# Top-32 attention with a highway layer: the 32nd value joins the common maximum, and GpSimd's part of a step is ordered anew

## The chip, the cores and the metric

The kernel runs on one core of a Trainium2 chip. The metric is the device time of one execution in microseconds (us), of the slowest core, which is here the only one. Five engines work side by side, each in the order of its own queue: TensorE (PE in the profile, its weight loads PEld), VectorE (DVE), ScalarE (ACT), GpSimd (POOL) and SyncE (SP), which here issues DMAs. They wait for each other by semaphores.

## The reference

Attention over 8 batches and 8 heads of 576 queries and keys (64 numbers each), in which only the 32 largest scores of a row count, followed by a highway layer over 4608 tokens of 512 numbers:

```python
scores = scale * np.matmul(q, k.transpose(0, 1, 3, 2))
kth = np.partition(scores, -32, axis=-1)[..., -32:-32 + 1]
scores = np.where(scores >= kth, scores, -1000000000.0)
attn = np.exp(scores - np.max(scores, axis=-1, keepdims=True))
x = np.matmul(attn / (np.sum(attn, axis=-1, keepdims=True) + 1e-09), v)   # then tokens x 512
H = np.maximum(x @ w_h, 0.0)
T = 1.0 / (1.0 + np.exp(-(x @ w_t + b_t)))
out = T * H + (1.0 - T) * x
```

Only the 32nd largest score of each row and its largest are needed, not the sorted list.

## The kernel before

**Units and steps.** A unit is 128 rows of scores: one head and one of four full blocks of 128 queries, or two heads and the remaining 64 queries. There are 288 units in 144 pairs, 18 pairs to a batch. The main loop calls `step(i)` for i = 0 to 142, and `finish` handles the last pair. Every engine's instructions run in the order in which the program writes them; there is no planner, so a line moved in `step` is moved in the queue of its engine.

**The 32nd largest value.** For each unit VectorE takes the eight largest of each of six segments of 96 scores (L353, `cand`, twelve instructions a pair). `refine` (L366 to L382) makes from them a threshold that is at or below the 24th largest value and near it: a maximum and a minimum of neighbouring segments (`high` L366, `low` L368), the negated `high` (`neg` L370), the eight largest of `low` and of `neg` for each unit (L373, L376, `en`), and their combination into a column of `cand` (L378). L382 is a maximum over `cand` in two groups: it writes the largest score (TOP) and the threshold (THR) of both units into `wall`. ScalarE then compares all scores with the threshold (L397, `masks_of`), which gives a mask and a count of the row (`csum`). PE adds the mask onto the scores in PSUM, so that all scores above the threshold sink (L410), and VectorE takes the eight largest of what remains (L420, `below`). With the count it is known which of the nine values, threshold and eight followers, is the 32nd: L426 compares nine constants with the count (`hits`: one 1 and eight 0), GpSimd multiplies these with the nine values (L436, `pick_a`), and VectorE sums the nine products (L439, `pick_b`) into the column KTH of `wall`.

**The use of it.** GpSimd's L391 (`biases`) multiplies TOP and KTH with factors for ScalarE's functions; the program makes it wait for VectorE's last keeping instruction of the step. For the first unit of a pair ScalarE makes the exponentials (L416) and a large value for every score above the 32nd (L443, `above`), and VectorE takes their minimum (L450). For the second GpSimd compares the scores with the 32nd (L454, `above_one`, `ro`), and VectorE multiplies (L460). When five or more passes of the layer wait for GpSimd, L454 is left out and VectorE does both at once (L465). SyncE's DMAs transpose the result, and PE multiplies it with v.

**Stages side by side.** Step i holds, of pair i+1, the segments (L353) and `refine`; of pair i, L420, L416, L426, L436 and L439; of pair i-1, L443, L454, L450 and L460; of pair i-3, the product with v; and PE starts the scores of pair i+2 (L309 and L318; L326 and L335 for the remaining 64 queries) in the buffer that pair i leaves.

**The layer.** When a block of queries is complete, `norm` takes it over: VectorE adds a constant to the sums (L557) and takes reciprocals (L559), and GpSimd scales (L564). GpSimd casts it by a DMA (L582), SyncE transposes it by another (L587), PE multiplies with the weights, and ScalarE evacuates the products (L609, L633). GpSimd makes three more passes over 128x512 or 128x256 numbers (L610, L611, L624), and a DMA of its own queue adds the results (L694, `do_add`). Other DMAs of that queue load v and the weights (L176, L182, L187, L213). The passes stand in a list, `pool_work`; `do_work` takes from its front what fits in the width that it is given. In `step`, the order on GpSimd is L391 of the step before, L454, the passes, L436, then DMAs, then L391. The evacuation of the layer's product stands ahead of `do_work` and appends the passes that it allows.

**Flags.** At the end `finish` checks on the chip that each 32nd value is positive, that each largest value is in a safe range and that the threshold lay where it should; otherwise a slower path computes everything again.

Of the kernel before, what the change touches and what calls it, by code (L numbers as in the profile page):

```python
# [10 lines left out]
ALU = mybir.AluOpType  # L11
# [15 lines left out]
def kernel(  # L27
# [68 lines left out]
    for jj in range(NPK):  # L96
        nc.vector.memset(pidx[:, jj : jj + 1], S - 2.0 * (TOP_K - jj))

    TOP, THR, KTH = 0, 1, NPK + 1
    wall = consts.tile([P, NU + 2, NPK + 2], FP32)  # L100
    fac = consts.tile([P, 2, 2], FP32)
    nc.vector.memset(fac[:, :, 0], -scale)
# [6 lines left out]
        nc.vector.memset(en[:, 0, :, 0:1], 3.0e38)  # L109
        ends.append(en)  # L110
    csum = consts.tile([P, NU], FP32)
    nc.vector.memset(wall[:, 0:2, KTH : KTH + 1], 0.0)

    def kth(u):
        return wall[:, u + 2, KTH : KTH + 1]
# [6 lines left out]

    cands = []
    for i in range(4):
        cand = consts.tile([P, 2, 8, 8], FP32, name=f"cand{i}")
        nc.vector.memset(cand[:, :, NSEG:, 0:1], -3.0e38)
        cands.append(cand)
    NM = 4
    masks = []
# [228 lines left out]
    def refine(g, cand):  # L358
        u0, u1 = pairs[g][0], pairs[g][1] + 1
        en = ends[g % NE]  # L360
        one = cand[:, :, 0:NSEG:2, :]
        two = cand[:, :, 1:NSEG:2, ::-1]
        high = cpool.tile([P, 2 * HALF], FP32, name="high")
        low = cpool.tile([P, 2 * HALF], FP32, name="low")
        neg = cpool.tile([P, 2 * HALF], FP32, name="neg")
        nc.vector.tensor_tensor(high[:].rearrange("p (s k r) -> p s k r", s=2, r=8), one, two, ALU.max)  # L366
        yield
        nc.vector.tensor_tensor(low[:].rearrange("p (s k r) -> p s k r", s=2, r=8), one, two, ALU.min)  # L368
        yield
        nc.vector.tensor_scalar(neg[:], high[:], -1.0, None, ALU.mult)  # L370
        yield
        for s in range(2):
            nc.vector.max(en[:, 0, s, 1:9], low[:, s * HALF : (s + 1) * HALF])  # L373
            yield
        for s in range(2):
            nc.vector.max(en[:, 1, s, 0:8], neg[:, s * HALF : (s + 1) * HALF])  # L376
            yield
        nc.vector.scalar_tensor_tensor(  # L378
            out=cand[:, :, :, 1], in0=en[:, 1, :, 0:8], scalar=-1.0, in1=en[:, 0, :, 0:8], op0=ALU.mult, op1=ALU.min
        )  # L380
        yield
        nc.vector.tensor_reduce(  # L382
            wall[:, u0:u1, TOP : THR + 1],
            cand[:, :, :, 0:2].rearrange("p s r k -> p s k r"),
            mybir.AxisListType.X,
            ALU.max,
        )
        yield

    def biases(g):  # L390
        return nc.gpsimd.tensor_tensor(be[:, g], wall[:, 2 * g : 2 * g + 2, TOP : KTH + 1 : KTH - TOP], fac[:], ALU.mult)  # L391

# [22 lines left out]
        return e  # L417

    def below(u, ps):
        nc.vector.max(wall[:, u, THR + 1 : KTH], ps)  # L420


    def hits(pair):
# [7 lines left out]
        )  # L431
        return hit

    def pick_a(pair, hit):
        u0, u1 = pair[0], pair[1] + 1
        nc.gpsimd.tensor_tensor(hit[:], hit[:], wall[:, u0:u1, THR:KTH], ALU.mult)  # L436

    def pick_b(pair, hit):
        nc.vector.tensor_reduce(wall[:, pair[0] + 2 : pair[0] + 4, KTH], hit[:], mybir.AxisListType.X, ALU.add)  # L439
# [12 lines left out]
    def above_one(u, sc):  # L452
        r = epool.tile([P, S], BF16, name="ro")
        nc.gpsimd.tensor_scalar(r[:], sc, kth(u), None, ALU.is_ge)  # L454
        return r
# [93 lines left out]
    def ffn_pieces(b, qt, xs):  # L549
        nh, ng, w = shape_of(qt)  # L550
        st = dict(b=b, qt=qt, xs=xs)
        blocks.append(st)

        def norm():
            xs3 = xs[:, 0 : nh * DE].rearrange("p (h e) -> p h e", e=DE)
            rinv = cpool.tile([P, H], FP32, name="rinv")
            nc.vector.tensor_scalar(rinv[:, 0:nh], xs3[:, :, D], 1e-9, 2.0, ALU.add, ALU.mult)  # L557
            yield
            nc.vector.reciprocal(rinv[:, 0:nh], rinv[:, 0:nh])  # L559
            x = xpool.tile([P, dm], FP32, name="x")  # L560
            st["x"] = x

            def scaled(e):
                e.tensor_tensor(  # L564
                    x[:, 0:w].rearrange("p (h d) -> p h d", h=nh),
                    xs3[:, :, 0:D],
                    rinv[:, 0:nh].unsqueeze(2).to_broadcast([P, nh, D]),
                    ALU.mult,
                )
                if by_dma:  # L570
                    casts.append(cast)
                else:
                    ready.extend([xt, hh, tt])

            pool_work.append((scaled, w))
            yield

        by_dma = isinstance(b, int) and units[-1][0:2] > (b, qt + 2)

        def cast():  # L580
            xb = xpool.tile([P, dm], BF16, name="xb")
            nc.gpsimd.dma_start(xb[:, 0:w], st["x"][:, 0:w])  # L582
            return partial(turn, xb)

        def turn(xb):
            st["xT"] = fpool.tile([P, n_g, P], BF16, name="xT")
            nc.sync.dma_start_transpose(st["xT"][:, 0:ng, :], xb[:, 0:w])  # L587
            flying.append(b)
            ready.extend([hh, tt])

        def xt():
            ps = fps.tile([P, 512], FP32, tag="fp", name="fp")
            for g in range(ng):
                nc.tensor.transpose(ps[:, g * P : (g + 1) * P], st["x"][:, g * P : (g + 1) * P], ident_f[:])
            xT = fpool.tile([P, n_g, P], BF16, name="xT")
            st["xT"] = xT
            psv = ps[:].rearrange("p (g j) -> p g j", j=P)
            return lambda: nc.scalar.copy(xT[:, 0:ng, :], psv[:, 0:ng, :])

        def hh():  # L600
            ps = fps.tile([P, 512], FP32, tag="fp", name="fp")
            project(ps, qt, st["xT"], wh, False)
            h2 = hpool.tile([P, dm], FP32, name="h2")
            s1 = xpool.tile([P, dm], FP32, name="s1")
            st["h2"], st["s1"] = h2, s1
            x = st["x"]

            def evac():
                nc.scalar.activation(h2[:, 0:w], ps[:, 0:w], AF.Relu)  # L609
                pool_work.append((lambda e: e.tensor_add(s1[:, 0:w], h2[:, 0:w], x[:, 0:w]), w))  # L610
                pool_work.append((lambda e: e.tensor_sub(h2[:, 0:w], h2[:, 0:w], x[:, 0:w]), w))  # L611

            return evac

        def tt():
            ps = fps.tile([P, 512], FP32, tag="fp", name="fp")
            project(ps, qt, st["xT"], wt, True)
            if by_dma:
                flying.pop()
            t = fpool.tile([P, dm], FP32, name="tt")  # L620
            h2, s1 = st["h2"], st["s1"]

            def gated(e):
                ins = e.tensor_mul(h2[:, 0:w], h2[:, 0:w], t[:, 0:w])  # L624
                if e is nc.gpsimd:
                    adds.append((s1[:, 0:w], h2[:, 0:w], partial(store, b, qt, s1)))
                else:
                    e.tensor_add(s1[:, 0:w], s1[:, 0:w], h2[:, 0:w])
                    store(b, qt, s1)
                return ins  # L630

            def evac():
                nc.scalar.activation(t[:, 0:w], ps[:, 0:w], AF.Tanh)  # L633
                pool_work.append((gated, w))

            return evac

        return norm
# [136 lines left out]
    def step(i):  # L775
# [25 lines left out]
        if prev:  # L801
            pu, ps_ = pairs[i - 1], st[i - 1]
            ps_["r"] = [above(pu[0], ps_["sc"][0])]
            ps_["r"].append(above_one(pu[1], ps_["sc"][1]) if len(pool_work) < (3 if last_steps else 5) else None)
        if late:
            late.pop(0)()
        if back:
# [2 lines left out]
            st.pop(j)  # L810
        spare(8 if i + 2 >= NG or units[pairs[i + 2][0]][1] < nfull or po["n"] else 3)
        ev = prep_filler() if to_prep and (i <= SPB or (len(to_prep) > 15 - k_in or len(layers) > 2) and i % 2) else None
        do_work(nc.gpsimd, 2 * dm if prev and ps_["r"][1] is None else dm)
        segs(i + 1, 2 * NSEG)
        if live:
            below(pr[0], st[i]["ps"][0])
# [31 lines left out]
            ps_["et"][s] = transposes(ep)  # L848
            return ins

        for _ in range(2):
            next(ra, None)
        if live:
            hit = hits(pr)
            pick_a(pr, hit)
        added = bool(adds or casts)
        if adds:
            do_add(i)
# [3 lines left out]
            todo_v.pop(0)()  # L862
        if todo_v and (i < 5 or added and i <= SPB):
            todo_v.pop(0)()
        for _ in range(5):
            next(ra, None)
        if live:
            pick_b(pr, hit)
        next(ra, None)
        masked(0)  # L870
        for _ in ra:
            pass
        scaling = norms.pop(0)() if norms else iter(())
        next(scaling, None)
        last = masked(1)
        if live:
            after(biases(i + 1), last)
# [65 lines left out]
    def finish():  # L943
# [49 lines left out]
        hit = hits(pr)  # L993
        ep, _ = keep_min(pu[0], old["e"][0], relu)
        old["et"][0] = transposes(ep)
        nc.vector.tensor_tensor(hit[:], hit[:], wall[:, pr[0] : pr[1] + 1, THR:KTH], ALU.mult)
        pick_b(pr, hit)
        x2 = xps.tile([P, 3 * BANK], FP32, tag="x", name="xs")
        cur["et"] = [etpool.tile([P, nck, P], BF16, name="et") for s in range(2)]
# [13 lines left out]
        yb = xs_of(nfull, 0, n)  # L1013
        project(bank(x1, 0), ya["qt"], ya["xT"], wh, False)
        do_work(nc.vector, NG * dm)
        nc.vector.scalar_tensor_tensor(cond[:], wall[:, 0:NU, THR + 1], ABOVE, wall[:, 0:NU, THR], ALU.mult, ALU.add)
        while stores:
            stores.pop(0)[1]()
        sure(2, cond[:], 1.0)
# [119 lines left out]
```

## Time and profile before

| what | value |
|---|---|
| three runs | 806.29, 806.73, 807.61 us; median 806.73 |
| profiled execution | 806.17 us |
| span of its instructions | 804.5 us |
| busy: PE, DVE, ACT, POOL | 686.7, 772.8, 757.2, 559.9 us |
| DVE instructions | 4020 |
| POOL instructions | 712 |
| mean granted clock of PE | 0.996 |

The profile is one execution, recorded by the hardware. A page sums it up; further views list groups of instructions of one line (busy time, mean length of one in ns, idle time of the engine before them and what ended it), who waited for whom (total, times, longest), the chain of waits that ended last, and the timeline: start, length, engine, line, operation, what is written and read, how often, and in brackets the idle time before it. A time without a unit is in us. An instruction's line in kernel.py is written L382; `cand<-xs` means that `cand` is written and `xs` read.

### The profile page before, as it was taken

What the parts mean: (1) busy time and instruction counts of PE and PEld (TensorE: products, weight loads), DVE (VectorE), ACT (ScalarE), POOL (GpSimd) and SP (SyncE); (2) the same over time, 40 slices, a digit from 0 to 9 for tenths busy, and PEclk for the clock granted to TensorE, in tenths of its full rate; (3) what the DMA queues carried; (4) which work ended last, traced back from release to release, by engine and by line L of the source; (5) the groups of instructions that cost most, each with busy time, mean ns of one, the idle gap of its engine ahead of it and who ended that gap; (6) DMA issues with size and microseconds to landing.
All of it is one profiled execution on the core that took longest, in us unless ns stands there. A gap on an engine that the chain in (4) does not pass through costs nothing.

```text
span 804.5 us, 20583 instructions
## 1 busy us (share of the span) xinstructions
PE 686.7 (85%) x6369; PEld 494.7 (61%) x6459; DVE 772.8 (96%) x4020; ACT 757.2 (94%) x1401; POOL 559.9 (70%) x712
## 2 busy tenths in 40 slices
PE   7889998888888888888987889888888888988884
PEld 5666766566666666566665666666666566665662
DVE  5999999999999999999999999999999999999996
ACT  5999999999999999999999999999999999999984
POOL 2666867777777767777767776777776777766750
PEclk9999999999999999999999999999999999999998
DMA  6789968996799667998669766898767996555653
GB/s 121 87 137 159 134 116 140 141 143 93 140 152 148 108 96 137 154 131 125 102 135 159 125 113 107 150 156 126 112 121 136 160 124 109 90 106 110 108 90 88
DMA packets 346359, 100.37 MB, mean 125 GB/s; under 512 B 330624, under 2 KB 338432, under 8 KB 346240
## 3 DMA queue, kind: packets, MB, share of 16 engines
q1 hardware_dynamic: 291024, 79.16, 54.1%
q0 software_dynamic: 53536, 19.34, 22.6%
q8 instruction: 53, 0.87, 0.4%
q10 hardware_dynamic: 1680, 0.46, 0.3%
q14 instruction: 66, 0.54, 0.2%
HBM read 31.72 MB, written 9.44 MB: 51 GB/s over the span
## 4 chain that ended last, share of the span: by engine, by line
ACT 37%; DVE 32%; PE 23%; DMA 4%; issue 3%; SPq 1%; another core or an unknown queue 0%; DVEq 0%; ACTq 0%
ACT m L397 15%; DVE wall L420 12%; DVE cand L353 9%; ACT e L416 7%; ACT sc L348 6%; PE pso L278 5%; ACT r L443 4%; PE xs L309 4%; PE xs L326 3%; DVE ep L450 3%; DMA xT<-xb 3%; PE fp L522 3%; PE xs L410 3%; PE pso L494 2%; ACT xs L508 2%
## 5 line engine op out<-in xcount | busy, mean ns | idle before, releaser
L353 DVE MAX8 cand<-xs 128x8 f32<-128x96 f32 x1728 | 297.5, 248 | 11.4 <-PE xs L335 6.2
L278 PE MATMUL pso<-cst,ident_b 128*128 128x252 bf16 x1841 | 246.8, 272 | 42.8 <-ACT xs L508 40.4
L454 POOL TENSOR_SCALAR ro<-sc,wall 128x576 bf16<-128x576 f32 x135 | 232.8, 1724 | 0.0
L416 ACT ACTIVATE e<-sc,be 128x576 bf16<-128x576 f32 x288 | 226.5, 787 | 0.1
L278 PEld LDWEIGHTS <-ident_b 128*128 128x128 bf16 x1841 | 173.4, 98 | 81.4 <-issue 49.5
L420 DVE MAX8 wall<-xs 128x8 f32<-128x576 f32 x288 | 204.3, 751 | 5.6 <-PE xs L410 3.5
L309 PE MATMUL xs<-kT,qT 64*128 64x256 f32 x1024 | 145.3, 400 | 30.6 <-DVE high L366 26.2
L348 ACT COPY sc<-xs 128x1152 f32<-128x1152 f32 x144 | 161.0, 1118 | 0.7 <-DVE cand L353 0.6
L309 PEld LDWEIGHTS xs<-kT,qT 64*128 64x128 f32 x1024 | 93.0, 186 | 61.3 <-issue 37.6
L397 ACT ACTIVATE m<-xs,wall 128x576 int8<-128x576 f32 x144 | 107.4, 746 | 18.2 <-DVE wall L382 17.1
L436 POOL TENSOR_TENSOR hit<-hit,wall 128x18 f32<-128x18 f32 x143 | 32.4, 227 | 121.2 <-DVE hit L426 114.0
L397 ACT ACTIVATE m<-sc,wall 128x576 int8<-128x576 f32 x144 | 111.4, 773 | 0.0
L443 ACT ACTIVATE r<-sc,be 128x576 bf16<-128x576 f32 x143 | 109.9, 769 | 0.0
L410 PE MATMUL xs<-m,ident_b 128*128 128x512 bf16 (+1 forms) x512 | 92.7, 274 | 17.3 <-ACT m L397 15.2
L494 PEld LDWEIGHTS <-et 128*128 128x128 bf16 (+1 forms) x1600 | 68.6, 100 | 19.2 <-issue 3.5
L391 POOL TENSOR_TENSOR be<-wall,fac 128x4 f32<-128x4 f32 x144 | 29.2, 203 | 72.5 <-DVE ep L460 53.7
L410 PEld LDWEIGHTS <-ident_b 128*128 128x128 bf16 x576 | 51.7, 97 | 44.8 <-issue 24.1
L494 PE MATMUL pso<-vb,et 128*128 128x65 bf16 (+1 forms) x1600 | 74.4, 194 | 4.2 <-DMA et<-ep 0.3
L450 DVE TENSOR_TENSOR ep<-e,r 128x576 bf16<-128x576 bf16 x143 | 64.6, 452 | 0.2 <-ACT r L443 0.2
L318 PEld LDWEIGHTS xs<-kd,qT 128*128 128x128 f32 x256 | 38.1, 188 | 42.5 <-issue 42.1
L318 PE MATMUL xs<-kd,qT 128*128 128x128 f32 x256 | 62.5, 326 | 0.0
L460 DVE TENSOR_TENSOR ep<-e,ro 128x576 bf16<-128x576 bf16 x135 | 60.7, 449 | 0.0
(127 smaller groups left out, 1028.9 us busy)
## 6 DMA issues: line engine op xcount, KB each, us to landing
kin<-in_k_dram SPq DMA_DIRECT2D x64, 128.0 KB, 2.9
qin<-in_q_dram SPq DMA_DIRECT2D x62, 128.0 KB, 3.1
out_dram<-s SPq DMA_DIRECT2D x30, 256.0 KB, 2.8
s<-h POOLq DMA_DIRECT2D x29, 256.0 KB, 4.0
et<-ep SPq DMA_TRANSPOSE x286, 3.3
xb<-x POOLq DMA_DIRECT2D x30, 128.0 KB, 3.0
vb<-in_v_dram POOLq DMA_DIRECT2D x28, 128.0 KB, 4.8
vb<-in_v_dram POOLq DMA_DIRECT2D x24, 64.0 KB, 3.1
```

The lines of the kernel that those rows point to most:

```text
L278: nc.tensor.matmul(po["t"][:, 4 * DE : BANK], ident_b[:], cst[:, 0 : BANK - 4 * DE], start=True, stop=True, skip_group_check=True,)
L309: nc.tensor.matmul(ps[:, mo + n0 : mo + n0 + 256], qT[r : r + D, hp, qs : qs + P], kT[r : r + D, hp, n0 : n0 + 256], start=(n0 == 0), stop ...
L318: nc.tensor.matmul(ends, qT[:, hp, qs : qs + P], kd[:, hp, :], start=True, stop=True)
L348: nc.scalar.copy(sc[:], both)
L353: nc.vector.max(cand[:, s, :], sc[:, s * SEG : (s + 1) * SEG])
L397: nc.scalar.activation(m1[:].bitcast(I8)[:, 1 : 2 * S : 2], ps, AF.Sign, bias=wall[:, u, THR : THR + 1], scale=ABOVE, accum_out=csum[:, u ...
L410: nc.tensor.matmul(ps[:, s0:s1], ident_b[:], m1[:, s0:s1], start=False, stop=True, skip_group_check=True)
L416: nc.scalar.activation(e[:], sc, AF.Exp, bias=tb(u), scale=scale)
L420: nc.vector.max(wall[:, u, THR + 1 : KTH], ps)
L443: nc.scalar.activation(r[:], sc, AF.Relu, bias=eb(u), scale=BIGK)
L454: nc.gpsimd.tensor_scalar(r[:], sc, kth(u), None, ALU.is_ge)
L494: nc.tensor.matmul(pso[r0 : r0 + ql, col : col + DE], ets[s][:, c, gi * P2 : gi * P2 + ql], vb[:, h, vc, :], start=(c == 0), stop=(c == nc ...
```

## The change

Four edits, in the lines of the kernel before:

- `wall` gets the columns TOP, KTH, THR, LOW (the eight followers). `cand` gets a ninth row. L382's maximum runs over nine rows and three columns, TOP, KTH and THR, instead of eight and two: 54 numbers into 6, where it was 32 into 4.
- L439, the sum, goes. GpSimd's product (now `pick`) is written into the KTH column of the next pair's `cand`, and L382's maximum over nine rows takes the one that isn't zero. L426 moves behind the two L376, and the product with it. On GpSimd the product therefore stands behind the step's DMAs, which were behind it. On VectorE the order after L376 is L426, L378, L450, L382 (which now waits for GpSimd), L460.
- The constant of `norm` (L557) is added by GpSimd, right behind the product; the reciprocal (L559), behind L460, waits for it.
- `do_work` is called in `step` only if `pool_work` had something before the step's evacuation (always in the last eight steps); two passes in one step need more than one such.

```diff
-    TOP, THR, KTH = 0, 1, NPK + 1
+    TOP, KTH, THR, LOW = 0, 1, 2, 3
...
-    nc.vector.memset(wall[:, 0:2, KTH : KTH + 1], 0.0)
...
-        cand = consts.tile([P, 2, 8, 8], FP32, name=f"cand{i}")
-        nc.vector.memset(cand[:, :, NSEG:, 0:1], -3.0e38)
+        cand = consts.tile([P, 2, NPK, 8], FP32, name=f"cand{i}")
+        nc.vector.memset(cand[:, :, NSEG:, :], -3.0e38)
...
-            out=cand[:, :, :, 1], in0=en[:, 1, :, 0:8], scalar=-1.0, in1=en[:, 0, :, 0:8], op0=ALU.mult, op1=ALU.min
+            out=cand[:, :, 0:8, THR], in0=en[:, 1, :, 0:8], scalar=-1.0, in1=en[:, 0, :, 0:8], op0=ALU.mult, op1=ALU.min
...
-            wall[:, u0:u1, TOP : THR + 1],
-            cand[:, :, :, 0:2].rearrange("p s r k -> p s k r"),
+            wall[:, u0:u1, TOP:LOW],
+            cand[:, :, :, TOP:LOW].rearrange("p s r k -> p s k r"),
...
-    def pick_a(pair, hit):
-        u0, u1 = pair[0], pair[1] + 1
-        nc.gpsimd.tensor_tensor(hit[:], hit[:], wall[:, u0:u1, THR:KTH], ALU.mult)
+    def pick(pair, pen, cand):
+        nc.gpsimd.tensor_tensor(cand[:, :, :, KTH], pen[:], wall[:, pair[0] : pair[1] + 1, THR:], ALU.mult)
...
-            nc.vector.tensor_scalar(rinv[:, 0:nh], xs3[:, :, D], 1e-9, 2.0, ALU.add, ALU.mult)
+            nc.gpsimd.tensor_scalar(rinv[:, 0:nh], xs3[:, :, D], 1e-9, 2.0, ALU.add, ALU.mult)
...
+        old = len(pool_work)
         if late:
             late.pop(0)()
...
-        do_work(nc.gpsimd, 2 * dm if prev and ps_["r"][1] is None else dm)
+        if old or last_steps:
+            do_work(nc.gpsimd, 2 * dm if prev and ps_["r"][1] is None and old > 1 else dm)
...
-        for _ in range(2):
-            next(ra, None)
-        if live:
-            hit = hits(pr)
-            pick_a(pr, hit)
         added = bool(adds or casts)
...
-        for _ in range(5):
+        for _ in range(7):
             next(ra, None)
         if live:
-            pick_b(pr, hit)
+            pick(pr, hits(pr), st[i + 1]["cand"])
+        scaling = norms.pop(0)() if norms else iter(())
+        next(scaling, None)
         next(ra, None)
         masked(0)
         for _ in ra:
             pass
-        scaling = norms.pop(0)() if norms else iter(())
-        next(scaling, None)
         last = masked(1)
```

`finish` keeps the sum (L439) for the last pair. The generator `ra` is `refine`: seven calls of `next` reach the second L376, the eighth L378, the rest L382.

More of the change, by code (lines that the diff above doesn't have):

```diff
@@ L390, in biases @@
     def biases(g):
-        return nc.gpsimd.tensor_tensor(be[:, g], wall[:, 2 * g : 2 * g + 2, TOP : KTH + 1 : KTH - TOP], fac[:], ALU.mult)
+        return nc.gpsimd.tensor_tensor(be[:, g], wall[:, 2 * g : 2 * g + 2, TOP:THR], fac[:], ALU.mult)
     def mask_count(u, ps):
@@ L419, in below @@
     def below(u, ps):
-        nc.vector.max(wall[:, u, THR + 1 : KTH], ps)
+        nc.vector.max(wall[:, u, LOW:], ps)
     def hits(pair):
@@ L995, in finish @@
         old["et"][0] = transposes(ep)
-        nc.vector.tensor_tensor(hit[:], hit[:], wall[:, pr[0] : pr[1] + 1, THR:KTH], ALU.mult)
+        nc.vector.tensor_tensor(hit[:], hit[:], wall[:, pr[0] : pr[1] + 1, THR:], ALU.mult)
         pick_b(pr, hit)
@@ L1015, in finish @@
         do_work(nc.vector, NG * dm)
-        nc.vector.scalar_tensor_tensor(cond[:], wall[:, 0:NU, THR + 1], ABOVE, wall[:, 0:NU, THR], ALU.mult, ALU.add)
+        nc.vector.scalar_tensor_tensor(cond[:], wall[:, 0:NU, LOW], ABOVE, wall[:, 0:NU, THR], ALU.mult, ALU.add)
         while stores:
```

## The prediction

> **What bounds the kernel now.** I read the page first: its busy shares, then the chain that ended last.
>
> ```profile
> span 804.5 us, 20583 instructions
> PE 686.7 (85%) x6369; PEld 494.7 (61%) x6459; DVE 772.8 (96%) x4020; ACT 757.2 (94%) x1401; POOL 559.9 (70%) x712
> ACT 37%; DVE 32%; PE 23%; DMA 4%; issue 3%; SPq 1%; another core or an unknown queue 0%; DVEq 0%; ACTq 0%
> ```
>
> DVE and ACT are both nearly full, and the chain changes between ACT, DVE and PE. So a nanosecond taken from DVE counts only in steps where DVE ends last. The next view is therefore DVE's timeline through one ordinary step (start, length, instruction):
>
> ```profile
> 341.29 2.07 DVE L353 MAX8 cand<-xs 128x8 f32<-128x96 f32 x12 [0.23 <-PE xs L318]
> 343.28 1.41 DVE L420 MAX8 wall<-xs 128x8 f32<-128x576 f32 x2
> ...
> 344.72 0.20 DVE L368 TENSOR_TENSOR low<-cand 128x48 f32<-128x48 f32 x1
> 344.83 0.17 DVE L426 TENSOR_TENSOR hit<-pidx,csum 128x18 f32<-128x18 f32 x1
> 344.92 0.18 DVE L370 TENSOR_SCALAR neg<-high 128x48 f32<-128x48 f32 x1
> 345.02 0.26 DVE L373 MAX8 en<-low 128x8 f32<-128x24 f32 x2
> 345.20 0.25 DVE L376 MAX8 en<-neg 128x8 f32<-128x24 f32 x2
> 345.37 0.15 DVE L439 TENSOR_REDUCE wall<-hit 128x2 f32<-128x18 f32 x1
> 345.48 0.19 DVE L378 SCALAR_TENSOR_TENSOR cand<-en 128x16 f32<-128x16 f32 x1
> 345.57 0.45 DVE L450 TENSOR_TENSOR ep<-e,r 128x576 bf16<-128x576 bf16 x1
> 345.94 0.21 DVE L382 TENSOR_REDUCE wall<-cand 128x4 f32<-128x32 f32 x1
> 346.06 0.45 DVE L460 TENSOR_TENSOR ep<-e,ro 128x576 bf16<-128x576 bf16 x1
> ```
>
> The next step's first L353 starts at 346.43 (L460's 346.06 and 0.37), a step of 5.14. Instructions overlap their neighbours by about 0.08, so an instruction costs the distance between starts (0.11 for L439), not its length. PE at the same place:
>
> ```profile
> 344.84 1.13 PE L309 MATMUL xs<-kT,qT 64*128 64x256 f32 x8 [0.54 <-DVE high L366]
> 345.90 0.49 PE L318 MATMUL xs<-kd,qT 128*128 128x128 f32 x2
> ```
>
> The scores that the next L353 reads end at 345.90 + 0.49 = 346.39, and L353 starts at 346.43. They start when L420 has freed the buffer, ahead of everything that is edited here. So PE and DVE finish together: time saved on DVE behind L420 buys nothing here, time added counts in full. How often the end depends on the joint maximum (L382) is in the chain of waits in order of time, where it stands 60 times (first and last shown), and in the table of waits:
>
> ```profile
> 13.55 0.22 DVE wall L382
> ...
> 764.96 0.13 DVE wall L382
> ```
>
> ```profile
> ACT m L397 <- DVE wall L382: 17.1, 47, 1.0
> ```
>
> ACT's masks wait for that maximum 47 times. What decides this change is therefore when L382 can run.
>
> **The change part by part.** L439 goes, once in each of 143 steps, 0.11 each. L426 moves behind L376. Shifting the rows: L376 at 345.11, hit 345.28 to 345.45, L378 345.39, L450 345.48 to 345.93, L382 could start at 345.85 instead of 345.94. But L382 now also waits for GpSimd's product, and that one's place is new:
>
> ```profile
> 341.04 0.19 POOL L391 TENSOR_TENSOR be<-wall,fac 128x4 f32<-128x4 f32 x1 [0.45 <-DVE ep L460]
> 341.21 1.72 POOL L454 TENSOR_SCALAR ro<-sc,wall 128x576 bf16<-128x576 f32 x1
> 342.91 1.26 POOL L624 TENSOR_TENSOR h<-h,tt 128x512 f32<-128x512 f32 x1
> 345.08 0.23 POOL L436 TENSOR_TENSOR hit<-hit,wall 128x18 f32<-128x18 f32 x1 [0.91 <-DVE hit L426]
> 345.60 0.93 POOL L694 DMA_DIRECT2D s<-h  x1 [0.30 <-POOL hit L436]
> ```
>
> The product starts 0.08 after the hit's end (345.00 to 345.08) and takes 0.23, before, while DVE runs MAX8 with one input. Afterwards it would run from 345.53 to 345.76 and be in time, were GpSimd free to read. But at 345.53 DVE is in L450, with two inputs from SBUF, right behind L378 with two. The trace has that situation once in each direction, at the end of the kernel and where a layer pass ran late (an L391 has a mean of 203 ns in the third row):
>
> ```profile
> 781.79 1.53 DVE L465 SCALAR_TENSOR_TENSOR ep<-sc,wall,e 128x576 bf16<-128x576 f32 x2
> 782.68 0.71 POOL L391 TENSOR_TENSOR be<-wall,fac 128x4 f32<-128x4 f32 x1 [1.64 <-DVE ep L465]
> L391 POOL TENSOR_TENSOR be<-wall,fac 128x4 f32<-128x4 f32 x144 | 29.2, 203 | 72.5 <-DVE ep L460 53.7 <-DVE wall L382 10.8 <-DVE ep L465 5.3
> ```
>
> ```profile
> 183.11 0.49 DVE L366 TENSOR_TENSOR high<-cand 128x48 f32<-128x48 f32 x1
> 182.26 1.27 POOL L610 TENSOR_TENSOR s<-h,x 128x512 f32<-128x512 f32 x1 [0.60 <-ACT h L609]
> ```
>
> In the first, GpSimd's 0.20 became 0.71: it ended at 783.39, 0.07 behind the second L465 (781.79 + 1.53 = 783.32). In the second, DVE's L366 waited for a pass that was running (end 183.53) and ended at 183.60. Who comes second waits for the whole instruction. Where a rule speaks to this: the Trainium skill, SBUF — State Buffer, section Who interferes with whom, says that a DVE instruction with two SBUF inputs and a GpSimd instruction that reads SBUF exclude each other, and that the first to issue keeps the ports to its end. By it the product waits out L450, as these two rows do; were two-input DVE work free of it, the sum would be that of the rival without a block.
>
> So the product ends about 0.09 behind L450 (0.07 as in that row, and 0.02 for 18 elements against 4): 345.93 + 0.09 = 346.02. L382 starts 0.05 later, the step in which L439 followed L436 (345.31, 345.37): 346.07, against 345.94. It also grows from 32 elements in 4 groups to 54 in 6:
>
> ```profile
> L382 DVE TENSOR_REDUCE wall<-cand 128x4 f32<-128x32 f32 x144 | 29.5, 205 | 0.1
> L439 DVE TENSOR_REDUCE wall<-hit 128x2 f32<-128x18 f32 x144 | 22.2, 154 | 0.0
> ```
>
> Between these, 14 elements and two groups cost 51 ns; L368 against L426 (0.20 for 48, 0.17 for 18) gives 1 ns an element. So 22 elements cost 0.02 to 0.08; I take 0.06. Its result, and with it L460, the next L353 and ACT's masks, come 0.13 + 0.06 = **0.19 later** in a step without a hole.
>
> How many steps pay: at least the 60 passes of the chain, 60 x 0.19 = 11.4; at most all, 143 x 0.19 = 27.2. I take 79, 15.0: the 60, and some 19 where DVE and PE end together as above and the chain went by PE. The others have a hole (0.23 in the first row) or wait for ACT.
>
> GpSimd's DMA issues now stand ahead of the product, and what is queued behind them is the product, the constant, L391 and L454:
>
> ```profile
> L694 POOL DMA_DIRECT2D s<-h x36 | 33.2, 922 | 9.3 <-POOL hit L436 9.3
> L187 POOL DMA_DIRECT2D vb<-in_v_dram x28 | 27.2, 972 | 7.5 <-issue 7.5
> L582 POOL DMA_DIRECT2D xb<-x x37 | 23.1, 624 | 10.4 <-POOL hit L436 10.4
> L564 POOL TENSOR_TENSOR x<-xs,rinv 128x512 f32<-128x512 f32 x31 | 32.4, 1045 | 0.0
> ```
>
> From one L391 to the product: 0.19 + 1.72 + 1.26 + 0.29 + 0.97 = 4.43 with a column of v (0.29 is the idle time before an issue, below), 4.39 with an add (0.30, 0.92); the blocked product would end 4.98 after 341.04, so 0.23 of its own still fits. In the four early steps with two DMAs and a pass it is 0.19 + 1.72 + 1.04 + 0.29 + 0.62 + 0.29 + 0.97 = 5.12, some 0.4 too late. Steps without a hole are shorter than this one, and a few more are late by 0.1. I take +3.0 (ends: 0, and 0.3 for each of the 64 adds and columns, 19).
>
> The constant (L557) leaves DVE. Where it met the issue of a column of v it took 0.47:
>
> ```profile
> 361.58 0.47 DVE L557 TENSOR_SCALAR rinv<-xs 128x8 f32<-128x8 f32 x1
> 361.11 0.96 POOL L187 DMA_DIRECT2D vb<-in_v_dram  x1 [0.29 <-issue]
> L557 DVE TENSOR_SCALAR rinv<-xs 128x8 f32<-128x8 f32 x31 | 6.8, 218 | 0.0
> L557 DVE TENSOR_SCALAR rinv<-xs 128x4 f32<-128x4 f32 x7 | 1.1, 160 | 0.0
> ```
>
> The 31 of full blocks have a mean of 218, the undisturbed small ones 160: 31 x 0.058 = 1.8, of which I take -1.6; the rest of the 6.8 overlaps its neighbours or stands before a hole. On GpSimd it is one small instruction, between 0.10 and 0.25, in the time in which L391 waits for L460 anyway (0.45 idle above); at nothing, or 38 x 0.2 = 8 at the worst if it met L460.
>
> The layer passes: the program's order on GpSimd differs in its passes only in steps 31 to 56; elsewhere old work is waiting anyway. It removes the pass that came with its evacuation (182.26 above, 0.60 idle, L366 longer by 0.29): -0.5, between -1.5 and +1. The projections and transposes there move by a step with their order kept. The loss of one memset and the new column order cost nothing; GpSimd's L391 has 4 elements as before.
>
> Sum: 15.0 + 3.0 - 1.6 - 0.5 = +15.9. The profiled execution took 806.17 (span 804.5 and 1.7 around it), so 822.1; its like by the median of the three runs, 806.73, is **822.6 us**.
>
> **The rivals.** (a) *The product restarts only when L450 has ended*: it ends 0.23 behind it, not 0.09, so 0.33 a step: 79 x 0.33 + 0.9 = +27, **833.7**. For: 0.71 is one row. Against: that row.
> (b) *GpSimd comes first*: L450 waits for the product (345.76) and ends 0.31 behind it (0.45 less the 0.14 that L366 did not lose), so that L382 starts at 345.99: 0.05 + 0.06 = 0.11 a step, 79 x 0.11 + 0.9 = +9.6, **816.3**. Against: L450 starts 0.05 ahead. The Trainium skill, SBUF — State Buffer, section Who interferes with whom, says that the issue order decides who blocks; no run here shows both orders for this pair.
> (c) *No block, but late DMAs*: L382 at 345.85, its result 0.03 earlier, worth 60 x 0.03 = 1.8; the issues delay the product by 0.3 in some 20 steps: +6.0 - 1.8 - 2.1 = +2.1, **808.8**.
> (d) *Faster*: the reads of an 18-element product slip in between L378 and L450. Then L382 starts 0.09 earlier, and with 0.03 for its growth ACT's masks come 0.06 earlier: 60 x 0.06 = 3.6, and 2.1 as above, and 0.4 for what else the constant takes: -6.1, **800.6**. It decides where the product's end in the records lies before L450's. For it: 47 waits of ACT. Against: both rows of the block.
> (e) *The change does not do what it says*: so it is with the passes, which begin as before outside steps 31 to 56; that is in the sum, at 0.5.
>
> **How the numbers follow.** Forecast 0.53, (a) 0.10, (b) 0.12, (c) 0.12, (d) 0.13. Range 806 to 836: it leaves out (d) and the end of (a), where L382 grows by 0.08 as well. Faster by over 0.2% (1.6 us, about what a measurement of this kernel can tell): (d) and 0.02 of (c), 0.15; within it 0.05 of (c); slower 0.80.
>
> **What would show it.** Right: GpSimd's product longer than 0.23 in most steps and ending just behind L450; L382 idle before it, waiting for GpSimd, about 0.15 in most of 143 steps; a 5.14 step grown to about 5.33; L382 near 260 ns; no L557 on DVE. Wrong: a product of 0.23 that ends inside L450 (d), or an L450 of over 0.6 (b). If the product is short but starts behind DMA issues, it is (c).

## The result and the profile after

The changed kernel takes **830.21 us** (median of six runs, 829.76 to 832.66) where the kernel before took 806.51 (six runs, 805.63 to 807.61): a ratio of 1.0299, 95% interval 1.0285 to 1.0314, so slower by some 24 us. Forecast were 822.6, a range of 806 to 836, and "slower" with 0.80. The sign and the range held; the time lies 7.6 us above the forecast.

Lines move by one to two: L353, L382, L436, L450, L460 and L391 of the kernel before are L352, L381, L434, L448, L458 and L390 now; the negation L370 is L369. First the page of the kernel after:

```profile
span 828.0 us, 20567 instructions
PE 698.5 (84%) x6369; PEld 496.5 (60%) x6459; DVE 783.1 (95%) x3838; ACT 762.1 (92%) x1401; POOL 595.9 (72%) x749
DVE 40%; PE 20%; ACT 17%; POOL 16%; issue 5%; DMA 1%; SPq 0%; POOLq 0%; DVEq 0%; ACTq 0%
```

GpSimd, absent from the chain before, has 16% of it now, and ACT's share fell from 37% to 17%. The timeline of VectorE in the step that corresponds to the one shown before, and GpSimd's beside it:

```profile
356.46 0.16 DVE L425 TENSOR_TENSOR hit<-pidx,csum 128x18 f32<-128x18 f32 x1
356.57 0.19 DVE L377 SCALAR_TENSOR_TENSOR cand<-en 128x16 f32<-128x16 f32 x1
356.67 0.45 DVE L448 TENSOR_TENSOR ep<-e,r 128x576 bf16<-128x576 bf16 x1
357.24 0.25 DVE L381 TENSOR_REDUCE wall<-cand 128x6 f32<-128x54 f32 x1
357.40 0.45 DVE L458 TENSOR_TENSOR ep<-e,ro 128x576 bf16<-128x576 bf16 x1
357.77 0.59 DVE L352 MAX8 cand<-xs 128x8 f32<-128x96 f32 x3
```

```profile
355.99 0.93 POOL L692 DMA_DIRECT2D s<-h  x1 [0.31 <-POOL h L622]
356.71 0.50 POOL L434 TENSOR_TENSOR cand<-hit,wall 128x18 f32<-128x18 f32 x1
```

The product starts 0.09 behind the comparison's end, takes 0.50 where it took 0.23, and ends at 357.21, 0.09 behind L448 (357.12). L381 starts 0.03 later: 0.57 after L448's start, where it was 0.37. The step has 5.28 instead of 5.14. The groups and the table of waits say how general that is:

```profile
L434 POOL TENSOR_TENSOR cand<-hit,wall 128x18 f32<-128x18 f32 x143 | 70.3, 492 | 77.8 <-DVE hit L425 72.9 <-DVE cand L377 3.9
L369 DVE TENSOR_SCALAR neg<-high 128x48 f32<-128x48 f32 x144 | 37.3, 259 | 0.0
L381 DVE TENSOR_REDUCE wall<-cand 128x6 f32<-128x54 f32 x144 | 36.1, 251 | 18.8 <-POOL cand L434 2.6
```

```profile
ACT m L396 <- DVE wall L381: 36.8, 86, 1.2
```

The product has a mean of 492 ns over all 143 steps (over 300 ns in 138 of them, and the usual end is 0.09 behind L448's), L381 one of 251 (205 before) behind 18.8 us of idle time, and the masks wait 86 times, not 47. One row wasn't expected: the **negation**, which the change doesn't touch, went from 180 to 259 ns. Where that sits is seen in a step with a column of v (one of the 28 loads of that form on GpSimd's queue, L187 before and L186 now), VectorE first, then GpSimd:

```profile
344.74 0.19 DVE L367 TENSOR_TENSOR low<-cand 128x48 f32<-128x48 f32 x1
344.86 0.65 DVE L369 TENSOR_SCALAR neg<-high 128x48 f32<-128x48 f32 x1
344.97 0.55 DVE L372 MAX8 en<-low 128x8 f32<-128x24 f32 x2
345.55 0.27 DVE L375 MAX8 en<-neg 128x8 f32<-128x24 f32 x2
```

```profile
344.56 0.96 POOL L186 DMA_DIRECT2D vb<-in_v_dram  x1
```

The negation ends at 345.51, the issue at 345.52; the L372 behind it wait along. L367, with two inputs inside the same issue, keeps its 0.19.

Step by step (from one start of L352 to the next, the same step in both): the 28 steps with a column are longer by 12.3 us together, 0.45 in the median; the other 115 by 11.4, of which 58 are longer by 0.10 to 0.30 (10.6 together) and 40 differ by under 0.06.

### The profile page after: what moved, and what is told of

The parts are those of the page before. It is cut to its first block, busy times and chain, and to the rows that moved or that the text cites. A ratio compares the mean times of both kernels' runs of the same rounds, so it can differ in the third digit from the quotient of the medians.

```text
span 828.0 us, 20567 instructions
## 1 busy us (share of the span) xinstructions
PE 698.5 (84%) x6369; PEld 496.5 (60%) x6459; DVE 783.1 (95%) x3838; ACT 762.1 (92%) x1401; POOL 595.9 (72%) x749
## 4 chain that ended last, share of the span: by engine, by line
DVE 40%; PE 20%; ACT 17%; POOL 16%; issue 5%; DMA 1%; SPq 0%; POOLq 0%; DVEq 0%; ACTq 0%
DVE wall L419 17%; ACT m L396 11%; DVE cand L352 9%; POOL cand L434 5%; POOL ro L452 4%; PE pso L277 4%; PE xs L325 3%; PE xs L308 3%; POOL h L622 3%; PE xs L409 3%; DVE wall L381 3%; PE fp L520 2%; PE pso L492 2%; DVE neg L369 2%; POOL s L692 2%
## 5 line engine op out<-in xcount | busy, mean ns | idle before, releaser
L352 DVE MAX8 cand<-xs 128x8 f32<-128x96 f32 x1728 | 296.6, 247 | 6.9 <-PE xs L317 3.1
L452 POOL TENSOR_SCALAR ro<-sc,wall 128x576 bf16<-128x576 f32 x134 | 230.4, 1719 | 0.0
L434 POOL TENSOR_TENSOR cand<-hit,wall 128x18 f32<-128x18 f32 x143 | 70.3, 492 | 77.8 <-DVE hit L425 72.9
L409 PE MATMUL xs<-m,ident_b 128*128 128x64 bf16 (+1 forms) x514 | 95.4, 274 | 31.4 <-ACT m L396 29.5
L390 POOL TENSOR_TENSOR be<-wall,fac 128x4 f32<-128x4 f32 x144 | 29.5, 205 | 106.5 <-DVE ep L458 86.5
L448 DVE TENSOR_TENSOR ep<-e,r 128x576 bf16<-128x576 bf16 x143 | 64.6, 452 | 0.4 <-ACT sc L347 0.2
L458 DVE TENSOR_TENSOR ep<-e,ro 128x576 bf16<-128x576 bf16 x134 | 60.2, 449 | 0.0
```

The source lines that it names most:

```text
L352: nc.vector.max(cand[:, s, :], sc[:, s * SEG : (s + 1) * SEG])
L409: nc.tensor.matmul(ps[:, s0:s1], ident_b[:], m1[:, s0:s1], start=False, stop=True, skip_group_check=True)
L434: nc.gpsimd.tensor_tensor(cand[:, :, :, KTH], pen[:], wall[:, pair[0] : pair[1] + 1, THR:], ALU.mult)
```

## The experiments

Main theory after the comparison: two hold-ups on what VectorE and GpSimd share, the product behind L448, the first keeping instruction (forecast), and the negation behind a column's issue (not forecast; this is theory B of the expectations). Rivals: the DMAs cost by delaying the product, as the prediction had it (theory A); the longer maximum, the constant or the passes cost by themselves. Ratios are to the kernel before in the same session (its medians there: 807.34 for runs 1 to 4, 806.77 for 5, 6, 7 and 10, 808.59 for 8, 9, 11 and 12), with 95% intervals; a ratio need not be the quotient of the medians.

**1. Loads behind the product**, adds and casts ahead:

```diff
-        elif todo_v:
-            todo_v.pop(0)()
...
             pick(pr, hits(pr), st[i + 1]["cand"])
+        if not added and todo_v:
+            todo_v.pop(0)()
...
```

> The changed kernel, with only the loads of GpSimd's queue (columns and ends of v, weights) put back behind the product; adds and casts stay ahead of it. Theory A (the sizes of the prediction: the product held up by the first keeping instruction costs 15 us, the DMAs ahead of it 3): 830.2 - 2 = 828. Theory B (the issue of a column of v holds up VectorE's negation, 28 times some 0.42): 830.2 - 11.5 = 818.7, and the negation has a mean near 182 ns, where it had 259. The product itself stays near 490 ns by both.

Measured: 830.09, ratio 1.0276 (1.0242 to 1.0310). By its time this spoke for A, but the negation was nearly free (mean 194), and a new wait stood in the table: the constant, right behind the product in the program, now stood behind the loads.

```profile
DVE rinv L557 <- POOL rinv L555: 6.5, 11, 1.0
```

So one edit had two effects, and the time alone doesn't decide. The next three runs do.

**2. Product in its old place**, DMAs behind it:

```diff
+        for _ in range(2):
+            next(ra, None)
+        if live:
+            pick(pr, hits(pr), st[i + 1]["cand"])
         added = bool(adds or casts)
...
-        if live:
-            pick(pr, hits(pr), st[i + 1]["cand"])
...
```

> The changed kernel with the comparison and the product back in their old place behind low, and all DMAs behind the product; the joint maximum over three columns, the constant on GpSimd and the later passes stay. By A and by B neither hold-up is left (product near 0.23, negation near 182 ns): 806.5 less 1.6 for the constant and 1 to 3 for the missing sum, near 804. Rival C (the longer joint maximum itself is the cost, 46 ns in each step that ends on it, and the passes put off cost 1.7): 806.5 + 3.6 + 1.7 - 1.6 = 810.

Measured: 815.38, ratio 1.0089 (1.0060 to 1.0117): two thirds of the loss are gone, the product is back at 228 ns, the negation at 186. What remains, 7 us (5 to 9 by the interval), is more than any of the theories had. Runs 5, 6 and 9 take it apart: the maximum +3.4, the constant +6.7, the passes -1.0; their 9.1 and the 7 agree as far as the intervals go.

**3. The late product alone**: DMAs behind it, constant and passes as before.

```diff
-        added = bool(adds or casts)
...
         if live:
             pick(pr, hits(pr), st[i + 1]["cand"])
+        added = bool(adds or casts)
...
-            nc.gpsimd.tensor_scalar(rinv[:, 0:nh], ...
+            nc.vector.tensor_scalar(rinv[:, 0:nh], ...
...
```

> The changed kernel with all DMAs behind the product, the constant back on VectorE and the passes as before: of the change only the late product and the joint maximum are left. Theory A: 806.5 + 15 = 821.5. Theory B: 830.2 - 11.5 for the negation, - 1.7 for one long step that the passes put off may have made, + 1.6 for the constant: 818.6. Rival C (the hold-up of the product is hidden in most steps, and only the DMAs ahead cost): 809 to 812.

Measured: 828.30, ratio 1.0254 (1.0225 to 1.0282), 20.5 us: dearer than all theories had it (negation 186, product 505). With the DMAs behind a product that ends at the step's end, GpSimd reaches the factors (L390) late; run 8 has the rows that speak for that.

**4. The negation with two inputs**:

```diff
+    minus = consts.tile([P, 1], FP32)
+    nc.vector.memset(minus[:], -1.0)
...
-        nc.vector.tensor_scalar(neg[:], high[:], -1.0, None, ALU.mult)
+        nc.vector.tensor_tensor(neg[:], high[:], minus[:].to_broadcast([P, 2 * HALF]), ALU.mult)
```

> The changed kernel, the negation done by another form of instruction: a product of two tensors (the second a column of -1, broadcast) where a tensor was multiplied with an immediate. high and low have two inputs and stand inside the same DMA issues with 0.19 to 0.20 us. Theory B: the negation is no longer held up by the issue of a column, mean near 200 ns: 830.2 - 11.5 + 1 = 820. Theory A: the DMAs cost by delaying the product, so that it stays at 830 to 832. Rival D: with two inputs the negation instead waits for GpSimd's passes, which end close to it, and the time goes above 832.

Measured: 823.28, ratio 1.0178 (1.0150 to 1.0206). Nothing is moved, only the form of one instruction is another, and some 9.8 us of the 24 are gone (1.0299 - 1.0178, of 806.5; 7 to 12 by the two intervals together, 7.8 by the medians of the two sessions). VectorE in a column step, GpSimd's issue below:

```profile
340.81 0.21 DVE L369 TENSOR_TENSOR low<-cand 128x48 f32<-128x48 f32 x1
340.94 0.21 DVE L371 TENSOR_TENSOR neg<-high,minus 128x48 f32<-128x48 f32 x1
```

```profile
340.62 0.97 POOL L188 DMA_DIRECT2D vb<-in_v_dram  x1
```

0.32 after the issue's start the negation takes 0.21. The column steps are now longer than before by 3.9 us together instead of 12.3. That is theory B; A and D are out.

**5. The joint maximum alone** (product early, DMAs behind, constant and passes as before), the constant alone, and the loads ahead alone, each from the kernel before. The maximum:

```diff
...
-            wall[:, u0:u1, TOP : THR + 1],
-            cand[:, :, :, 0:2].rearrange("p s r k -> p s k r"),
+            wall[:, u0:u1, TOP:LOW],
+            cand[:, :, :, TOP:LOW].rearrange("p s r k -> p s k r"),
...
```

> Of the change only the joint maximum over three columns (and with it no sum): product in its old place, DMAs behind it, constant on VectorE, passes as before. Theory A and B: the maximum is some 40 ns longer, its input is there in time; with the 79 steps that the prediction let pay, 79 x 0.04 = 3.2, and nothing for the sum, 0.11 a step, which lay beside PE: 807 + 3 = 810. With all 143 steps paying: 813. Rival F (the sum's 0.11 counts in each step): 143 x (0.04 - 0.11) = -10: 797.

Measured: 810.48, ratio 1.0042 (1.0029 to 1.0055), +3.4 us, as the 79 steps had it. F is out, and VectorE's timeline shows why a sum less gains nothing:

```profile
347.07 0.25 DVE L375 MAX8 en<-neg 128x8 f32<-128x24 f32 x2
347.35 0.19 DVE L377 SCALAR_TENSOR_TENSOR cand<-en 128x16 f32<-128x16 f32 x1
347.45 0.45 DVE L448 TENSOR_TENSOR ep<-e,r 128x576 bf16<-128x576 bf16 x1
347.81 0.24 DVE L381 TENSOR_REDUCE wall<-cand 128x6 f32<-128x54 f32 x1
```

L377 reads what L375 writes and starts 0.03 behind its end (347.32); before, the sum stood between them, and L378 started 0.28 after L376, as here. The sum had filled a gap that stays.

**6. The constant alone**:

```diff
-            nc.vector.tensor_scalar(rinv[:, 0:nh], ...
+            nc.gpsimd.tensor_scalar(rinv[:, 0:nh], ...
...
             pick_b(pr, hit)
+        scaling = norms.pop(0)() if norms else iter(())
+        next(scaling, None)
...
```

> The kernel before, with only the constant of the sums added by GpSimd, at the place in the program that the changed kernel gives it. The prediction: 1.6 less, 805.4. Rival G: in this kernel the DMAs stand ahead of the constant on GpSimd, so that the reciprocal waits for an issue of 0.62 to 0.97 in the steps that have one: up to 31 x 0.6 = +19, 807 to 825.

Measured: 813.64, ratio 1.0083 (1.0063 to 1.0103), **+6.7** where the forecast had -1.6. Rival G holds: the reciprocal waits for GpSimd.

```profile
L559 DVE RECIPROCAL rinv<-rinv 128x8 f32<-128x8 f32 x31 | 6.3, 202 | 8.1 <-POOL rinv L557 7.3
```

**7. The loads ahead alone**:

```diff
...
+        if not added and todo_v:
+            todo_v.pop(0)()
...
         for _ in range(2):
             next(ra, None)
         if live:
             hit = hits(pr)
             pick_a(pr, hit)
...
```

> The kernel before, with only the loads of GpSimd's queue moved ahead of the comparison and the product; product, sum, joint maximum and adds stay. Theory B (the issue of a column holds up the negation, and in these steps VectorE ends late as a whole): the negation grows from 180 to about 250 ns, and 28 x 0.35 to 0.45 come on top: 807 + 10 to 12.5 = 817 to 819.5. Theory A (a late product is what the loads cost): the sum waits for the product in the same steps, negation at 180, 28 x 0.3 at most: 807 to 815. Rival E (the column steps have a hole that takes the hold-up): 807 to 809.

Measured: 816.49, ratio 1.0118 (1.0096 to 1.0139), +9.5: 0.5 below B's range and above A's. The rows decide for B: the negation has a mean of 240 ns, the product keeps 228, and the sum waits for it 1.5 us in all.

```profile
L370 DVE TENSOR_SCALAR neg<-high 128x48 f32<-128x48 f32 x144 | 34.5, 240 | 0.0
```

**8. The changed kernel without constant and passes** (its diff is the second half of run 3's, and `do_work` as before):

> The changed kernel with the constant back on VectorE and the passes as before: joint maximum, late product and DMAs ahead of it are left. Against the kernel in which the DMAs stand behind the late product (828.3) it shows what their place is worth: theory A (as predicted) +3: 831; theory B with K (the negation +7 to +10, casts and adds that no longer push GpSimd's next step back -5 to -8): 828 to 832, with the negation again at 259. Against the changed kernel (830.2) it shows constant and passes together there: the prediction has -2.1 for them, so 832.3 here; if they are worth nothing where the DMAs stand ahead, 830.

(K is the idea that casts and adds ahead let GpSimd go on earlier; runs 11 and 12 test it in the kernel before.)

Measured: 833.56, ratio 1.0302 (1.0281 to 1.0323). Against 1.0299: constant and passes together are worth nothing there that these runs could tell (2 us or so). Against run 3: the DMAs' place costs some 3.9 us net (1 to 7 by the two intervals together). It holds the negation up again (267) and in return lets GpSimd go on; the row of the factors, run 3 first, then this one:

```profile
L390 POOL TENSOR_TENSOR be<-wall,fac 128x4 f32<-128x4 f32 x144 | 35.7, 248 | 34.8 <-DVE ep L458 17.2 <-DVE wall L381 10.5 <-DVE ep L463 3.0
```

```profile
L390 POOL TENSOR_TENSOR be<-wall,fac 128x4 f32<-128x4 f32 x144 | 29.5, 205 | 119.8 <-DVE ep L458 98.7 <-DVE wall L381 11.0 <-DVE ep L463 7.9
```

GpSimd stood ready before L390 for 119.8 us in all here, and for 34.8 in run 3. With the 9.8 of run 4 taken out, the place ahead is a gain of some 6 us. This is an estimate from four ratios, 2 to 10 us by their intervals together; no run shows the gain alone.

**9. The passes alone**: `do_work` only if something older waits.

> The kernel before, with only the later passes (a pass of the layer is not taken in the step whose evacuation allows it, if nothing older waits). The prediction: -0.5, between -1.5 and +1: 806.3. From the runs so far (the kernel with the early product, constant and passes, less the one with neither, +4.9, less the constant alone, +6.9): -2, 805. Rival J (the passes put off push a piece of the next batch's preparation into a late step): 808 to 810.

Measured: 807.14, ratio 0.9987 (0.9974 to 1.0000). The forecast's -0.5 lies inside; J is out.

**10. The maximum first**:

```diff
-        next(ra, None)
-        masked(0)
         for _ in ra:
             pass
+        masked(0)
```

> The kernel before, with only the joint maximum moved ahead of the first keeping instruction, so that its result comes some 0.37 earlier and everything else of VectorE stays. It asks whether the time of the joint maximum is what counts, as the prediction has it. If so: the 47 waits of ScalarE's masks (17.1 us) mostly go, and the 60 passes of the chain get shorter by up to 0.3: 807 - 8 = 799 or less. Rival H (the maximum then waits for the combination right ahead of it, and the transposing DMAs of the first keeping instruction start later): 806 to 811. Rival I (PE's scores end at the same time anyway, so no step ends earlier): 807.

Measured: 816.98, ratio 1.0114 (1.0093 to 1.0136): slower than any of the three had it. VectorE:

```profile
347.70 0.15 DVE L439 TENSOR_REDUCE wall<-hit 128x2 f32<-128x18 f32 x1
347.81 0.19 DVE L378 SCALAR_TENSOR_TENSOR cand<-en 128x16 f32<-128x16 f32 x1
348.04 0.21 DVE L382 TENSOR_REDUCE wall<-cand 128x4 f32<-128x32 f32 x1
348.16 0.45 DVE L450 TENSOR_TENSOR ep<-e,r 128x576 bf16<-128x576 bf16 x1
```

L382 starts 0.23 after the instruction whose result it reads, where an independent one follows at 0.09. VectorE's part of a step is longer by that 0.14, and the steps are longer by 0.10 in the median (0.13 in the 22 without a DMA), though the maximum comes earlier. ScalarE's masks still wait for it, 41 times and 19.3 us (47 and 17.1 before). So an earlier maximum bought nothing that shows, and a longer VectorE was paid for. What the later transposing DMAs of rival H add is not separated from this.

**11 and 12. What the place of casts and adds is worth in the kernel before**: the casts ahead of the comparison; casts and adds ahead, with the sum behind the maximum.

```diff
...
+        if casts and not adds:
+            turns.append((i + 2, casts.pop(0)()))
         for _ in range(2):
             next(ra, None)
...
```

> The kernel before, with only the casting DMAs moved ahead of the comparison and the product (adds and loads stay behind): a cast of 0.62 then ends before the comparison is done, and its block is transposed about 0.8 earlier. PE waits for transposed blocks in its layer products 10 times in the kernel before, 13.0 us of PE and its weight loads together. Theory K (those waits make some of the long steps, and the place of the casts in the changed kernel is a gain that lies inside its loss): 806.8 - 2 to - 5 = 802 to 805. Rival L (what follows waits for another engine anyway): 806 to 808. Rival B again (the issue of a cast also holds up the negation): 37 x 0.1 to 0.3, 810 to 818.

> The kernel before, with casts and adds ahead of the comparison and the product, loads behind, and the sum moved behind the joint maximum so that a product that an add has put off isn't waited for by it. Theory K: GpSimd is free for the factors and the comparison 0.9 earlier in 73 steps: 800 to 804. Rival M (a product that is put off meets the first keeping instruction, as in the changed kernel, and the factors wait for the sum, which now stands later): 807 to 815.

Measured: 813.07, ratio 1.0055 (1.0039 to 1.0072), and 815.03, ratio 1.0087 (1.0067 to 1.0107). Theory K falls in this kernel. Run 11 lies in the range of rival B, but not by B's reason: the negation has a mean of 185 ns, 5 more than before, 0.8 us over 144. In run 11 PE's waits for transposed blocks got longer, not shorter (6.3 us before):

```profile
PE fp L522 <- DMA xT<-xb: 10.5, 10, 2.6
```

Why they come later although they are cast earlier stays open, and with it most of run 11's loss. In run 12 the delayed product met L450 again in some steps, as M said (over 300 ns in 35 of 143):

```profile
L436 POOL TENSOR_TENSOR hit<-hit,wall 128x18 f32<-128x18 f32 x143 | 43.5, 304 | 63.6 <-DVE hit L426 52.3 <-DVE neg L370 10.5
```

None of the twelve beats the kernel before; the passes alone come level with it.

## Why the prediction was right, and where it was not

- **The block of the product** (right): predicted was an end 0.09 behind the first keeping instruction, L381 0.05 behind that, a step of 5.33 and 260 ns for L381; measured are 0.09, 0.03, 5.28 and 251. The Trainium skill, SBUF — State Buffer, section Who interferes with whom, gave the block, though not these sizes, and the trace agrees (492 ns in the mean).
- **How many steps pay** (right in sum): 79 were taken at 0.19, 15.0. Measured are 58 steps without a column, 10.6, and the 28 columns' share, 3.9 by run 4: 86 steps, 14.5. That the two sums lie so close is partly luck: the 79 were the 60 passes of the chain and 19 more by estimate, not these steps; and the 14.5 are what is left with the DMAs ahead, while with the DMAs behind (run 3) the late product and the longer maximum cost 20.5. What the 40 steps that hardly changed end on was not followed up.
- **"I take +3.0" for the DMA issues ahead of the product** (the step that failed, in size and in kind): the price was put on the product that comes late. It came through the negation instead: 12.3 less 3.9 = 8.4 by the steps, 9.8 by run 4 (7 to 12), 9.5 alone (run 7). The mechanism stood in a fence of the prediction, the constant of 0.47 inside a column's issue; it was used only for the constant that leaves, not for the next instruction of the same form that the issue would now meet. Not all of it was a loss: by runs 3, 4 and 8 the place ahead gives some 6 us back (the estimate above) if the product is late anyway; that this is by GpSimd's earlier factors is argued from its idle time.
- **"-1.6" for the constant** (failed): nothing, together with the passes, in the changed kernel (run 8), +6.7 alone. With the DMAs moved ahead the constant on VectorE is free of them already (run 8, beside 218 before), so that taking it away gains nothing:

```profile
L555 DVE TENSOR_SCALAR rinv<-xs 128x8 f32<-128x8 f32 x31 | 5.0, 162 | 0.0
```

- **The growth of L382, the sum and the passes** (right): 46 ns against 60, nothing for the sum, -1.0 (-2.1 to 0.0) against -0.5 for the passes alone.
- **"What decides this change is therefore when L382 can run"** (half right): the time lost there was lost, but, it seems, because everything behind it on VectorE is late too: run 10 makes the maximum earlier and VectorE longer, and is slower.
- Sum: 14.5 + 8.4 = 22.9 (the 10.6 and 12.3 of the steps, shared out by run 4) of the profiled execution's 23.5 (span 828.0 against 804.5). The rest is the net of single steps. The largest, of 7.21 at 245.8 and 1.71 longer than before, is of another kind: PE's scores took 2.08 there for eight matmuls instead of 1.13, and the granted clock of PE in that stretch was 0.50, against 1.00 in the same step before; why it fell is open. The row of the stretch (busy PE, PEld, DVE, ACT and POOL, then clock, DMA share and GB/s):

```profile
250.19:252.27 2.08, 2.08 (x10) 1.25 (x9) 0.98 (x4) 2.08 (x5) 1.55 (x4) 0.50 0.77 160
```

- Against the forecast's 15.9 the 23.5 are 7.6 more: 5.4 in the term of the DMA issues (8.4 for 3.0), 2.1 in constant and passes, 0.6 in the rest, less 0.5 in the block.

Rivals of the prediction: (a) falls by the end 0.09 behind L448, (b) by L448's unchanged 0.45, (c) and (d) by the 492 ns.

## What to carry to other kernels

When an instruction of GpSimd is moved, DMA issues included, look at which instructions of VectorE it will now lie beside, and price their forms from the rows where they met before. A short instruction between two dependent ones may fill a gap that stays when it goes; what is saved there is shown by the distance of the starts around it, not by its length. An edit that is meant to take work off one engine can cost more through the queue that it joins.

## What the runs showed of the hardware

- **The issue of a column of v on GpSimd (0.97) held up a VectorE `tensor_scalar` on fp32 in SBUF, but not a `tensor_tensor`, and only from some 0.3 us on.** Over all traces, a negation or constant that started up to 0.26 after such an issue kept its time (13 of 13), and one that started between 0.285 and 0.68 after it ended with the issue (104 of 104). Shorter or other issues did it less: of the negations that started from 0.29 on beside a cast (0.62) 22 of 65 were held, beside an add (0.92) 10 of 49. Where the negation was a `tensor_tensor` (run 4), none took over 0.21. The constant in run 3, and beside it the negation of 344.86 above (0.30 behind its issue, 0.65 long):

```profile
72.61 0.16 DVE L555 TENSOR_SCALAR rinv<-xs 128x8 f32<-128x8 f32 x1
```

```profile
72.35 0.97 POOL L186 DMA_DIRECT2D vb<-in_v_dram  x1
```

  The Trainium skill, SBUF — State Buffer, section Who interferes with whom, names `tensor_scalar` among the instructions that can take the port pair shared with GpSimd, and says that a `tensor_tensor` contends with GpSimd's reads alone; runs 4 and 7 agree.
- **A short VectorE instruction that read its neighbour's result started 0.14 later than an independent one**: 0.23 against 0.09 between the starts of L378 (16 elements) and its successor (32 elements, run 10). It is seen on this pair of lines; L377 in run 5, which starts 0.03 behind the end of L375, fits it.
